# Another table for the order of all operations of a sliding-window attention and cosine-MLP kernel

## The chip, the cores and the metric

One core of one Trainium2 chip. The engines are TensorE (PE, whose weight loads are shown apart as PEld), VectorE (DVE), ScalarE (ACT), GpSimd (POOL) and SyncE (SP); the last two issue the DMAs. The metric is device time in microseconds of one execution; a lower time is better.

## The reference, cut to what matters

Sliding-window attention with ALiBi slopes over 8 batches, 8 heads, 576 positions and 64 channels, followed by a two-layer network with g = h * cos(h) over all 4608 tokens.

```python
scores = scale * np.matmul(q, k.transpose(0, 1, 3, 2))
bias = slopes[:, None, None] * (-np.abs(rel).astype(np.float32))[None, :, :]
mask = (rel >= 0) & (rel < window)
scores = np.where(mask, scores + bias[None], -1000000000.0)
attn = np.exp(scores - np.max(scores, axis=-1, keepdims=True))
attn = attn / (np.sum(attn, axis=-1, keepdims=True) + 1e-09)
attn_out = np.matmul(attn, v)
x = np.ascontiguousarray(attn_out.transpose(0, 2, 1, 3)).reshape(B * S, H * D)
h = x @ w_in
g = h * np.cos(h)
out = (g @ w_out).astype(np.float32)
```

Here window is 128, w_in is 512 x 2048 and w_out 2048 x 512.

## The kernel before, in words

The program isn't written engine by engine. The function bass_alibi_sliding__then__act_gcu_kernel (L253) records 2842 operations with `op` (L115), each with its engine, what it reads and writes, and a function that issues its instructions. Then `follow` (L160) reads a table, the string TABLE, which gives one order for all operations; `emit` (L174) deals them out to the engines in that order and puts in the semaphore waits that the reads and writes require. So the table alone sets the order on each engine and on the two queues that issue DMAs. Each entry of the table is two bytes, a step from the entry before; its low 15 bits are an operation's number, and its high bit chooses DVE for the operations that can run on ACT or DVE.

The work is tiled in attention units and in chunks of tokens.

- A batch b has nine units: head pairs 0 to 3 with query half G=0, the same with G=1, and a tail of the last 64 queries. For a unit, `scores` (L518) multiplies keys with queries on PE (L539, the tail L529), `exps` (L581) takes the exponential on ACT (L598, L590), `mask` (L603) multiplies with the table EM of decay factors on DVE (L623, L611), `pv` (L627) multiplies with v on PE (L653 and L656, tail L640 and L642), `norm` (L673) divides on DVE (L694, L696), and the result goes transposed to xT, by PE and a copy (`x_pe`, L721, matmul L742, copy L751 to L753) or by a DMA transpose of SP (`x_dma`, L757).
- Queries and keys of batches 0 and 1 are loaded by POOL's DMAs (`load_qk`, L351; `load_first_q`, L359, over SP) and transposed on PE in pieces (`qk_transposes`, L469, matmuls L483, copies L500 on ACT and L501 on DVE). For batches 2 to 7 POOL loads them as they are (`load_nat`, L381, five DMAs at L385), and SP transposes each by two DMAs (`dma_transposes`, L392, L396 and L399). The tiles of q and of k have two buffers each, used by even and odd batches.
- `load_v` (L372, DMA at L375) loads v by blocks of 128 positions, again into two buffers. `load_w_in` (L406, L407) loads w_in in four blocks of 512 columns, `load_w_out` (L412, L413) w_out in four. All are issued by POOL.
- A chunk c is 512 tokens, nine in all. Chunk 0 multiplies with w_in in halves (`moe1_half`, L964, PE at L975), the others in full (`moe1`, L782) or with seven products in place of eight (`moe1_fast`, L859, L876). ACT takes the cosine, DVE multiplies. The products with w_out are `moe2` (L1161) for chunk 0 and `moe2_fast` (L1056, L1067) after, and stores go out over SP (L1095, L1168).
- `masks` (L458) makes EM: eight exponentials on ACT (L460, one for each head) and four copies on DVE (L465, each for two heads, which waits for both).

An engine's queue is strictly in order: an instruction that waits holds all that stand behind it. This also holds for the DMAs that SP and POOL issue. A buffer that is filled again waits for those who read what was in it.

The lines of `follow` that read an entry:

```python
at = (at + lo + 256 * hi) % 65536
o = self.all[at % 32768]
if isinstance(o.fn, dict):
    e = "dve" if at >= 32768 else "act"
    o.fn, o.eng = o.fn[e], (e,)
self.order.append(o)
```

Of the kernel before, what the change touches and what calls it, by code (L numbers as in the profile page):

```python
# [27 lines left out]


TABLE = (  # L30
    'c-nPV2Y6If7JmPfH!Wo*A%PHdEHqifjs=k}tV#(GFqBXPBn4$bu`FK_%_4*%1ObV(K#D*JSt&-E!h-'
    '0xDvPKfD@{Z`QYO7kX6D^JciMYzU|;fHUhcd1+;jf_Kj&N_3_w#jJy552L+3%Pc;zlP#H-yktj(-'
    'pEjqM{ck}PJwCrB3q-'
    '{9M;&d$5qHR9WADS}~;_2H1xbO#`q+wdtgon`B>6%HyG|f?3%VnDsdnr<5N0St5ZZ)?8zmXNGD<Zg2=y6N`U+Gy?'
    '$F$*GyJWJoN!r+3anTS_iMU&FrmJy)q1{k##U*rYHRJHq^Dy35b!Y@oPU}o$A?_9;n<O%5Xs0l2&{m^^1BgNm_9P'
    '~pqObs4C1TN&{Qy{6(86~%nA#%H5NW^O=4`d2vLnc~h(_}2&mQcz_^`@$G{b79x#rnLjt-93Hcj0-'
    'yv%|m2e+*e0cZK}!+72b)WUaJT8@pXD+fk0N6bOV1gB(Si4?NA5T2-'
    '!JB(zEKr!Mj%{>;HUNYjab!Z7$qCql;L3G!CjefR+FFk(bw73vr<2ntCbb8MB)_5dQYyf6J%<J=0tY;ul(MgN&rc'
    'O0s&EiG$uIcm#Y~Vab;v#yqnaVrE7GY>V-A}Btqa`;P_Nv&jvF#{*7WM`>VMkre&#)Wy?uO_aV#gax-'
    'm{4=v5trFP6j>R?Tw2c0rY#J*M(j<PaOY>o)>#w^hUa2)xJ2kX>J~-'  # L40
    '#3SczLYEI#)13`0UMgZCvSU&r@KXVhQx8AYHOt^~S#t385v1pL)39f1&X4(!RY_VSn%~;N7Le~0Vt5k)3C!7qncH'
    'Sb_KKyP6<WQBL=(H{om`}^2hwehkBNkN1f6-'
    '=6Jf`#n1*9F&|{#~8ip5b`?XFO3>mnmKg4fqM&X#D2BXTu`vb#MxEL-'
    '2=FZh<=U!>)?uhVjo~ev?pC0h90j^d!W2#$W>Vg}3Lez;yMB~`dF58D5!*GHZ4bkokcrZJo8XMBIs3+J`c0!*&!='
    'cNak2M(+9t6%k<c;_TI5&xT-;_~SjMe)zLQ?kr-'
    '9G)}so_oZgT~!nS)>B%(>F{i(nL<%Kma6dPT_kIY8xqVGm@6sSZY)QY;}3kyZHF!JjrNbPWohF6A1kpQae^Jz>4Y'
    'nMq|4ag_#Z%abX$X0Qx{bdg5-'
    'w!C^Sy0wzSSv6YO*7!5g5KOZPW>L)jeqDWi^PVfHiNt_&bV&I7<#pb?el1f*R3lvbBscPqQM6(|M=#E!7MQtWiEo'
    '^$q8jetWg{{laSk`ID;w6<lHL!It@CI3ZRWxET-dy=6bdfZi^BN)-'
    'kx6rkxYh^Af7Y$CX%W0qP@nf!;+_cuy#JAV$$(>L5)aS8M@n1a32RRL3Yb{W0a`!VJ8|o4{JEnxs(L});p(&v8a9'  # L50
    'u_yO{KZHL$YuW?tu(Sy-'
    '!vCGTmAdZpg4wXLtycpkG<<E5@OtDZg=!_1h1+Njmjw*z0aL)7QnhFOPv(elHPlI>oe%EXgvk}suL+RHI+l!oPEe'
    'ttc)y)KY7q-'
    'GO9HpEp~!82*s>_!_J5TR{@5f%EL7h^Wh(4l4fbO%j~jd783&`#My06C4>3;+Is6L%3tT|^hYe#$tr1&iB&6{dwW'
    'wmj!;Baz_4=p8Jja_9ps>tY{=<;GUvOwSAXGq+K`;>!KNrH|ImXY(ASTzHFN^apdvpSj*r6^VK)$8H@P=`NPcPO&'
    'XkYSBhFw`irt0gqb!LQPqlVQC7VwU?z)4yP6n<)+6xUk=rH29r)HJ=#nkkufV0J5o_@v9wsQWd0@&P$WT0e*0vOC'
    'WIl=#9la*x}LDtWaQG=0xl2(#f%Kz3QWi+K|tR$xwKh#_K~ywPUk>V_~X988-'
    'dL$7M*|kTUzrMQ~>ttJm@GYT>9QFLiQ#JGHIu^Q5UX9joXGsV+1N~s5tf4rg&Z0t843@yK)VUZ;eO{vvf>bj#_<{'
    'E{YJE13lG{)N}UY3D6Y>lsCkRX4ja{$9_e$IQETy;j`zD56VwIGwJ{vRRhIkkY72;<?OL;WxyDsbjLJ`d?#gik4L'
    '%OwvOj>3X-Yk5pe`ia}jeHouYwjx-lYe?zUO*6w~{=z!E<7?VOdoJcyIBk3;YN22T&Udsl*?z2EoT*eN`VQ(2lOw'  # L60
    '$ie!%Cd#CND}y^H-5G~apWoVM#%(x$>q1=4UeA7@v$>FHVpXpRNz-`z1w9-2S&rNI|0<^yIkuIxJ1&2qr-'
    'yn-P&*BAkwbEg<YgZWM`B<Ux7!?;yxT0hEB9Poq9_H<xB+6$<+&1*V*jXQ=!i##UhbBC-HxJ9b4f>O5FQM$GVlYY'
    '0;EzOMeT$+Oi@ir?~G>em;QF`Fb7Uw0-'
    ')DSUv5QX5E;wvHsQX@ok50m+CO*%wR0XM0gH$JNq(o?|pd}rcrfU%@Ny^NS$EwY}9WNlRrb}CwAb0!CyUIkX8zeE'
    't`lBMNi5`Z9289jS-byN0#8`Z0-K46!6u51NJvfI*I<pVOKD}#Bep<(EjKAJ>#OvyA?}aT-'
    'Eb<QtZWG>gAiq@nZu|-Z>5YIIxXgTPJ-Qv8(%8OF{x~utj?J<T~4~q=Mu!G!`B%o{U^X7EYfMjy|cFw5l`KlR}P!'
    'Ka8_mW<8uzKs|eA|5Ic*_e7cdlcU3q+K^v!GU5I4-4igxj^A<ASLge=;<iQSZL!w7=WR?W#-'
    'vXhCLeN@7x(>g+{qRDABl6lLS<Fw>!h`LQKaFe(HMu)ipAva=P&;AW;|7_8}?>Xa&1&CWqRI3oTyJm0VHkMj~b-'
    'KU~R;VLVn(IO$x|2XD-#Cwa~YvoxGM@0FUnOnlZXB(9|3jhMQu{ARUV7(DVnyPJ@o)_f&pP-'
    '0v1&I@q5tK0fHEZqW2B6vpePz;Nsr3p!)OwvLraMQ%IB0%b!Fk8kvD!^ICX(d5SU`>)JBl;A)3x!^A~*gA1H!Njk'  # L70
    '9bb31AJ#9jLnSFn5nJP8V+>6WI*{{9$K=-'
    'Ii4(}ekB>9rlTbz8;dAV@$vsGY#Mm*p3)v9cI)0mEeyn;9Sk1Ej+_{IEB=6m(OWM%qp|L4FkV=POcUwRSz4?%tjO'
    '!EE7%nJVFo1y$1xLEKDW3+%V*`a_(LEi!<eA{Ja22J?)4@RI|7PRIIN8a6UkTIrQNx^0MmIX}Gdse33v8*ibI3(}'
    'Q6!`hQq7VFL0TWDyL%1z)LEb|Fqa2QJsRyz<9M$)jGC(Gyq6mu#GUiIyWiMn}lrw_vC^2CnX65Kq(JOA5auqsW#('
    'az6gPr;3Fs3vS*iFTO!lleCE-fW~K`s@;f-'
    'DuL7*vWwMFvwo)YDYK%Ys!&lL=}a$qa_Dqe_$j$%4|P%7Sk&C^p7|E-05OoaEoQU{w(_HKhuIl)N)0L6E?If-ndQ'
    'f>bOkomPRMj6=zXYB;2Fs8S$=8>KAS9bxj%$jo92RQykW$_h$ynL-'
    ';1n|B~0C{NjJ5M;#~HD{_qDyS92ASr8Q=(}$hf?wlN8Dh7U35CEE3Rb4eZHcVrLB=YO&ys+EVM&F9-'
    '>_E|awkyN8>TE$>Y^ZLfm%hXRv?#4)t*Y5EYzr4%5w1xWK3uw7gWYn<tfyI;9|8HRZ>;#t145fwkp%W<gb}oO8Vt'
    ';%~TDI391Zd3iT@kVuEmcuME+!AOkCeh?Xh408{MGRAGcvK=>2_;SOCz;Xi5FXBMh@##BcNK~)Hu608vNLvl*BDH'  # L80
# [1244 lines left out]
```

## Time and profile before

| | |
|---|---|
| median of 3 runs | 300.12 us (299.69 to 300.17) |
| the profiled execution | 299.71 us |
| its span in the profile | 298.0 us |
| granted TensorE clock | 1.0 |

In a row of a group or of the timeline stand the start or the line, the time, engine, line of the kernel, operation, tiles (out<-in) and count. A row of the chain of waits gives start, length and what ran there. A row of the waits gives who waited, for whom, the total, how often and the longest. PE durations overlap: a matmul of 512 columns is shown with some 380 ns, though the next starts 216 ns after it, so rates are read from the start-to-start spacing.

### The profile page before, as it was taken

The numbers are of one execution on the slowest core, as the hardware profiler recorded it, in microseconds if no ns is written. First come the engines' busy times: TensorE is split into PE (matmuls) and PEld (weight loads), VectorE is DVE, ScalarE is ACT, GpSimd is POOL, SyncE is SP. The second block draws the span as 40 slices with busy tenths as digits, with TensorE's granted clock in tenths as the row PEclk, the third lists the DMA queues.
The fourth block names the chain that finished last, engine by engine and source line by source line (L and its number), as shares of the span: only waits on it lengthen the run. The fifth ranks groups of instructions, "written<-read, shape, count | busy, mean of one in ns | idle before, by whom it ended". The sixth has DMA issues, their size and how long they took to land.

```text
span 298.0 us, 7278 instructions
## 1 busy us (share of the span) xinstructions
PE 287.9 (97%) x2974; PEld 205.2 (69%) x2974; DVE 262.1 (88%) x522; ACT 222.1 (75%) x318; POOL 95.2 (32%) x122
## 2 busy tenths in 40 slices
PE   2899999999999999999999999999999999999996
PEld 2678845446874586458854788547768888888884
DVE  3879877599977999899999999999999999999972
ACT  5788878689757889688777878579778758778620
POOL 7997000599642303991195005000000000000000
PEclk9999999999999999999999999999999999999999
DMA  7999999999999994999999939973131400041033
GB/s 153 173 205 208 207 169 146 180 196 155 136 175 147 130 187 90 142 173 173 169 170 133 163 85 130 159 164 74 21 79 21 150 2 0 2 141 37 10 134 106
DMA packets 147729, 37.96 MB, mean 127 GB/s; under 512 B 133360, under 2 KB 146416, under 8 KB 147696
## 3 DMA queue, kind: packets, MB, share of 16 engines
q0 software_dynamic: 99344, 18.10, 79.7%
q1 hardware_dynamic: 48352, 19.41, 34.5%
q8 instruction: 23, 0.38, 0.5%
q14 instruction: 10, 0.08, 0.1%
HBM read 36.70 MB, written 9.44 MB: 155 GB/s over the span
## 4 chain that ended last, share of the span: by engine, by line
PE 94%; DVE 2%; POOL 1%; issue 1%; ACT 1%; POOLq 0%; DVEq 0%
PE ps L1067 33%; PE ps L782 24%; PE ps L876 11%; PE ps L539 5%; PE ps L975 5%; PE ps L1161 4%; PE ps L653 3%; PE ps L656 2%; PE ps L742 2%; PE ps L483 2%; PE ps L529 1%; DVE kt L501 1%; PE ps L640 1%; PE ps L642 1%; PE ps L1138 1%
## 5 line engine op out<-in xcount | busy, mean ns | idle before, releaser
L1067 PE MATMUL ps<-w_outb,gT 128*128 128x256 f16 x512 | 82.3, 273 | 0.0
L782 PE MATMUL ps<-xT,w_inb 128*128 128x512 f16 x336 | 82.2, 379 | 0.0
L787 ACT ACTIVATE cos<-ps,halfpi 128x512 f32<-128x512 f32 x84 | 54.9, 687 | 18.9 <-PE ps L782 13.9
L598 ACT ACTIVATE p<-ps 128x768 bf16<-128x768 f32 (+1 forms) x64 | 55.6, 915 | 11.5 <-PE ps L539 9.5
L791 DVE TENSOR_TENSOR gT<-ps,cos 128x512 f16<-128x512 f32 x84 | 54.5, 686 | 5.5 <-ACT cos L787 5.1
L1067 PEld LDWEIGHTS ps<-w_outb,gT 128*128 128x128 f16 x512 | 48.2, 98 | 12.5 <-issue 1.3
L782 PEld LDWEIGHTS ps<-xT,w_inb 128*128 128x128 f16 x336 | 31.7, 98 | 31.1 <-DVE gT L791 1.5
L375 POOL DMA_DIRECT2D vp<-in_v_dram x40 | 34.3, 892 | 53.1 <-PE ps L656 35.3
L1067 PE MATMUL ps<-wsum,gsum 128*128 128x256 f16 x256 | 38.5, 273 | 0.0
L623 DVE TENSOR_TENSOR p<-p,emask 128x768 bf16<-128x768 bf16 (+1 forms) x64 | 38.0, 615 | 0.3
L385 POOL DMA_DIRECT2D qnat<-in_q_dram x30 | 25.5, 918 | 23.9 <-DMA qt<-qnat 23.9
L1052 ACT ACTIVATE ob<-ps 128x512 f32<-128x512 f32 x33 | 19.6, 598 | 13.7 <-PE ps L1067 11.2
L385 POOL DMA_DIRECT2D knat<-in_k_dram x30 | 25.7, 948 | 9.3 <-DMA kt<-knat 7.0
L1067 PEld LDWEIGHTS ps<-wsum,gsum 128*128 128x128 f16 x256 | 23.2, 98 | 4.0 <-issue 0.5
L876 PE MATMUL ps<-xT,w_inb 128*128 128x256 f16 x132 | 24.8, 273 | 0.0
L696 DVE TENSOR_TENSOR xnats<-ps,rec 128x256 f16<-128x256 f32 x56 | 21.9, 420 | 0.5
L539 PE MATMUL ps<-qt,kt 64*128 64x128 bf16 (+1 forms) x320 | 20.1, 253 | 1.3 <-DVE kt L501 1.3
L653 PEld LDWEIGHTS ps<-vp,p 128*128 128x128 bf16 x256 | 16.0, 99 | 4.3 <-issue 1.0
L653 PE MATMUL ps<-vp,p 128*128 128x65 bf16 x256 | 18.9, 196 | 0.1
L1067 PE MATMUL ps<-wsum,gT 128*128 128x256 f16 x112 | 18.1, 273 | 0.0
L539 PEld LDWEIGHTS ps<-qt,kt 64*128 64x128 bf16 x320 | 11.9, 98 | 8.6 <-issue 3.6
L1161 PE MATMUL ps<-w_outb,gT 128*128 128x512 f16 x64 | 17.6, 380 | 0.0
(111 smaller groups left out, 478.0 us busy)
## 6 DMA issues: line engine op xcount, KB each, us to landing
out_dram<-ob SPq DMA_DIRECT2D x35, 256.0 KB, 2.7
vp<-in_v_dram POOLq DMA_DIRECT2D x32, 128.0 KB, 6.9
qnat<-in_q_dram POOLq DMA_DIRECT2D x24, 128.0 KB, 7.1
knat<-in_k_dram POOLq DMA_DIRECT2D x24, 128.0 KB, 10.8
w_inb<-in_moe_w_in_dram POOLq DMA_DIRECT2D x4, 512.0 KB, 10.5
w_outb<-in_moe_w_out_dram POOLq DMA_DIRECT2D x4, 512.0 KB, 21.8
gsum<-in_q_dram POOLq DMA_DIRECT2D x1, 576.0 KB, 15.5
gsum<-in_k_dram POOLq DMA_DIRECT2D x1, 576.0 KB, 17.6
```

The source lines that it names most:

```text
L375: op("pool", [lambda e, t=t, rows=rows: e.dma_start(vp[b % 2][0:rows, t, :, 0:64], v[b, :, 128 * t:128 * t + rows, :].rearrange("h p d -> ...
L385: fns.append(lambda e, t=t, rows=rows: e.dma_start(nat[which][b % 2][0:rows, t, :, :], src[b, :, 128 * t:128 * t + rows, :].rearrange("h p ...
L539: ins = e.matmul(ps[:, banks[x], c0:c1], keys_ap(b, x, pr, kc), query_ap(b, x, pr, qb, 128 * nb), start=c0 == 0 and (b, pr, G) not in seed ...
L598: op("act", lambda e: e.activation(P[i][:, :, 0:hi], src_[:, :, 0:hi], ACTF.Exp, scale=0.125), w=held + [("P", i)], occ=920 if G else 691, ...
L623: op("dve", lambda e: e.tensor_tensor(p, p, m, ALU.mult), r=[("EM", h0), ("EM", h1)] + ([] if G else [("EM2", h1)]), w=[("P", i)], occ=600 ...
L653: ins = e.matmul(o, P[i][:, x, d0:d0 + 128], V[:, kc, h, 0:65], start=True, stop=not two)
L782: op("pe", lambda e, kc=kc: e.matmul(ps[:, bank, :], w_in[:, kc, 128 * fc:128 * fc + 128], xT[:, kc, r0:r0 + CH], start=(kc == 0), stop=(k ...
L787: op("act", lambda e: e.activation(cosb[ci][:, :], ps[:, bank, :], ACTF.Sin, bias=halfpi[:, 0:1]), r=["halfpi"], w=[("B", bank), ("cos", c ...
L791: op("dve", lambda e: e.tensor_tensor(gT[gi][:, fc, :], ps[:, bank, :], cosb[ci][:, :], ALU.mult), r=[("cos", ci)], w=[("B", bank), ("g", ...
L876: op("pe", lambda e, i=i, kc=kc: e.matmul(ps[:, bank, 256 * i:256 * i + 256], left(kc, p0 + i), right(kc), start=(start and i == 0 and kc ...
L1067: op("pe", lambda e, t=t, p=p: e.matmul(ps[:, bank, 256 * t:256 * t + 256], left(p, slice(128 * t, 128 * t + 128)), right(p), start=(start ...
L1161: op("pe", lambda e, t=t, fc=fc, bank=bank: e.matmul(ps[:, bank, :], gT[gi][:, fc, 128 * t:128 * t + 128], w_out[:, fc, :], start=(fc == 0 ...
```

## The change

The string TABLE is replaced, and one line of `follow` is edited.

```diff
 TABLE = (
-    'c-nPV2Y6If7JmPfH!Wo*A%PHdEHqifjs=k}tV#(GFqBXPBn4$bu`FK_%_4*%1ObV(K#D*JSt&-E!h-'
...
+    'c-n1N30zZG_I@8(2nkt$fCW0XRYY60(^~u2|CAZESnG-l%BHN^PyrQ(DlS+SMJj?;L_t)LML{TtEN-'
...
 )
@@
             if isinstance(o.fn, dict):
-                e = "dve" if at >= 32768 else "act"
+                e = "dve" if at >= 32768 else o.eng[0]
                 o.fn, o.eng = o.fn[e], (e,)
```

Unpacked as `follow` does it (base 85, zlib, steps of two bytes), both tables name the same 2842 operations, and 2703 of the 2842 places hold another one. Every operation with a choice has "act" as its first engine. Of these, 13 change the engine: six go from ACT to DVE, seven from DVE to ACT; among the latter is the copy of the first group of batch 0's second piece of q. Counts by engine are PE 1860 in both, ACT 304 and 305, DVE 522 and 521, POOL 70, SP 86. The switches between Exp and Sin on ACT are 14 in both.

What the prediction speaks of, by engine (u0 to u7 are batch 0's units in their order, q1/k1 its first pieces, q2/k2 its second, "a" and "b" a piece's two groups):

```
ACT, from the start
before: EM2 EM6 cast EM3 EM0 EM1 EM5 q1a k1a EM4 EM7 exp u0 exp u1 q2b exp u2 exp u3 exp u4 exp u5 exp u6 x u0 x u2 x u3
after:  EM4 EM2 cast EM3 EM0 EM5 EM7 q1a EM1 k1a EM6 exp u1 exp u0 q2a q2b exp u2 exp u3 exp u4 exp u5 exp u6 x u1 x u2 x u3
DVE, from the first cast
before: cast q1b EM(2,3) k1b EM(6,7) EM(0,1) EM(4,5) mask u0 mask u1 q2a k2b k2a mask u2 mask u3 ...
after:  cast halfpi EM(2,3) vinit EM(4,5) Pt q1b ktail k1b vinit EM(0,1) EM(6,7) mask u0 mask u1 k2a k2b mask u2 mask u3 ...
PE, after the transposes of q2 and k2
before: scores u2 u3, pv u0 u1, scores u4 u5, pv u2 u3, scores u6, x u1 u0 u3 u2, scores u7, scores tail, w_in products
after:  scores u2 u3, pv u0 u1, scores u4 u5, pv u2 u3, scores u6, x u1 u0, scores u7, x u3 u2, one w_in product, scores tail, w_in products
POOL's DMAs
before: k1 [iota] q2 k2 v1 v0 v3 wi0 v2 wi1 wi2 wi3 q k v4 wo0-3 | batch 1's v1 v0 v3 v2 | nat q2 nat k2 | nat q3 | ...
after:  k1 q2 [iota] k2 v0 v1 v2 wi0 v3 wi1 wi2 wi3 q v4 k wo0-3 | batch 1's v0 v4 v1 | batch 2's v2 | batch 1's v2 v3 | batch 2's v1 | nat q2 nat k2 | batch 2's v3 | nat q4 | batch 2's v0 | nat q3 nat k3 ...
SP's DMAs
before: ... T q2, store, T k2, 2 stores, T q3, store o1, store, T k3, x tail, T k4, T q4, 2 stores, T k5, ...
after:  ... T q2, T k2, 3 stores, store o1, store, T q3, T k3, T q4, x tail, T k4, 3 stores, T k5, ...
```

In the last two lists "nat q2" is `load_nat` of q of batch 2 and "T q2" its DMA transposes; in the first part of POOL's list q and k alone are those of batch 1. Further back on POOL and SP most DMAs have other places too. On PE, groups of `scores` that stand directly behind another kind of matmul, or `qk_transposes` that do, are one more than before: 84 changes of kind in place of 82. The last 14 operations of PE are the same, as are the last 9 of SP.

More of the change, by code (lines that the diff above doesn't have):

```diff
@@ L30 @@
 TABLE = (
-    'c-nPV2Y6If7JmPfH!Wo*A%PHdEHqifjs=k}tV#(GFqBXPBn4$bu`FK_%_4*%1ObV(K#D*JSt&-E!h-'
[L32 to L80, printed above, removed]
@@ L81 @@
-    'GHNRFy;B3gs%n{7pj$fl+x7VWHhmHY6$LK<1t&5`BViq8BRfR0)!TR`@J<FZkbrVSDq@w=+*W79u-'
-    'AsdYv9Vyey(st|R(RU84Bg0wsI(4aO|@>6G)${!)5eW-e@5K<&=Z_fWO<s>k5KMFa_g&GrXJ7L|{Z-'
-    'kIjkN?mA0G*W>_y'
+    'c-n1N30zZG_I@8(2nkt$fCW0XRYY60(^~u2|CAZESnG-l%BHN^PyrQ(DlS+SMJj?;L_t)LML{TtEN-'
+    '=}or={ij=xrGtJYe#ju4ixB_!d!xd|kBFP#MP?)L6I=R4o|&ZV5uFEjxB5rfYRjH6iE@7gPHX!oFdl#jj8$=5!IH'
+    'mO=V_M!LB6aM3_8FXtCx;_(n|2~R-;?g$i%2a9p!|`<Mm(wK=72mz-CHeM6n%67t9sTW;dkVgO{5AF4zlrpd(69Y'
+    '`@^ioX;QlKQuKSL;|H=UFOvLS1%VV#-`tM1%UjfiB`Q~r<kLS;1mDUq2ezI04*+n1salZ`mk^4c5-'
@@ new lines @@
+    '&ZsB_{tx8$Bb1!Mf@@9w@)!?@^20`K|uHT*7~_XT!GFRMu8LHq(i5xqgvJjxC)FNZe$$L|KpU>T{HC>e{jleh+0R'
+    'yavfwI1|bw0#fF?Nmwt$~(l)2jt-Vr@Zs?q(y<|+UDuwciDB=v}qSO&m^_s(~%3gA4bLe3e(0OhS;J|dcIadbIGM'
+    't#-'
+    'JRcMq#r}{q_Jvjl*K2v<I2K(Y)bZqf`en~<^#$FWSnaT^K^IIcZ&+AEI~wJk!S^2YEjqoZ!BMver~O()lUw{+1hc'
+    'QTZPs6PJs(??w3kWlJc5}&w7q}G|MNg%^a%6_@BQ@;47%tY?_OTSgQG$##gpgTJoJW2r&Yp&fA|8e0{4{6ZrY{Q6'
+    'IyYb17rrB_fzj~{*hRkw^QYQGFD?ey;O<#y`fbag}^8Xb=?WMTD~E}pv({5o{{uggsexueGD$Vi))H;zw|lpNy0<'
+    '_d)s#S#BL;i7#*8DI@Y;wr5g?;?8@#Sf5=;xwS}0sCn=MT{)^;`^SgF;AS-A5+|-'
@@ new lines @@
+    'P2IX0$Ax?CFnm4mCF#=CX6p?%kzK{>5~K34(;_ij+AcGrHL3nUfA7H#R>57pr=Z2k!AKh6|Ca_#j@bY7d4oV_^@>'
+    '1lBVJzMwhi`hDOutyeGfHy*(>~rv&<WLq~L0(vO6w5FF{dmmP+aZ!-'
+    '#ArWTpuIk|^rbyXGa3Uf_ZS0?JWf9|@5~eUPOI+%l<l&p0~mDEVC*e{i#PDN(^u3sAW)!N-'
+    's#yoqFo};jCi8twes=rkUIvCQN11Nv8|tld)>Iu@UI^|+FV+_GvXKzL%#t^Lw7zBcnZzF#OT)&W$mjcV%H|D$tP&'
+    'wyR&mAe~+qA((H4d{$;63KjH3?_e?VfCGSdW`y)`HDilW+#iF+?9*4qeRuV)D1meyFep&x&qu|i%?|ig5I~FC0S@'
+    'Cl0{pZ%5JGW*rTXV!3o$C35z9^JMmVB^Rm;iN2j1u`FW%P!lokC;874<@8`-$aa(#0DyQq%6=5C+vO_}t%X!X|$-'
@@ new lines @@
+    '&)=F|Q?V@k)ROApvdBh#Uu52gN0;q$UtS-'
+    ';3&A_x?!H%eG*7HOb~AUPe~!S{QQs!|!^;hi1tJ&*orI_j>v7k2%W2-G@qu!+?k|rg-SvGezx%u#6Ta|(hBkQj=x'
+    'Gl_Hv}@T-'
+    '*sD&nz1hts0dF>$D@(EH$ECkvXs!$1OiE1e$pOOBI+I2<(UR9&FGZ^$=Qq2UrX$dFO6!)@fC3C8W5F>2{g;g*CJ2'
+    'ZvAj+)8<2PR)`yoyH7q=#0(prXqEVEIp04Lth5?8AlBDTM-'
+    '&w@_bd4fyy#jgd4(n<kxg;Ka=DhCQl!6g~E<3jZJ65B>$zA=@gUIIa&YGZ7kz~QL_}`o7pFa^azd5!lpz&>S)yv~'
+    'lg$;{U#yNq_V;*IVDV@A2n${f;<()J(R5m<m3KpvePAuP&g%7ig*ZgFj#eOX@Hz)FMjeFLFK({u7cTr$Pc=JNBwk'
+    'U!>=7F&ZA$%TvD2V^E+Mtp0z*oD!`lEbJrV`te+Z-cK3p-'
@@ new lines @@
+    'sO@86;r$coF|u6^#Ayj!Oj&|!Dxjy3s7J9f42cFIh$!gtq~Ke%y=l1QJqd*jFfJOFkbG<9M{d6zx+uSF|7{_xr<;'
+    'w3%<JhE05rDUzD(Hd9Q1Qo7^>jOE8Q*senvi`PLNz9QX<gTjki{In6Dm$5k1jv>2Zjh)CPJ2_5k-BLciaY$SZ^-'
+    'ZbaMyzz;PR~fovBFw0FtNPeY=H;hechR_KM#Zo?e7)DOu?QqLfS`8@DF(Ax9i9&hHR!%Siyq;?yjVbk*%k+*hSvy'
+    '5$W7)&*XCr#{3%d#7CL8%CeJlXg<~1LAy+I|WvTRpQcT^Pm58R??o}YGo(QBLW|u3Lk^F0)ksE9&^uj7#)R3%$8s'
+    'LKbJPQZh`R&ymck8E+G0CfAFmTi@z8>)$WEtskY0vttP&sDn`qn-RyEWgx}-S2erFV(7~7QP0*Ha``u6#Z-'
+    'OnXa%n9PQNFULrXG0s0?|@Zp4`=BYM{j*3UswAKb-'
@@ new lines @@
+    '|gKbZ|@^qv(?@FD&}P##(rOx7H840FaY{XleGASC^`HUou1-ZC;FDvTE4sAErDML6m8$o8)-'
+    'bVRg6MR)u`85tq$DO{bmE;&v7|EmW69y?>_!HSi|E8^e>;hYVJf8KLgHRY|B-'
+    '=F&Kg_eId!96k;vR|Xm(nNFM_3(wKKVB^c#{Ke>)A`ks^KN8+!Pv0Mn-j-'
+    'w#>#KR6Gh+k$bfeD(W09Ufa6HxvFRp$@M@(qUxE_&_QgT|lacoshZi2=^@Ic41Bze2p~SqAC}@NGmaI0sIq%H4k('
+    'nu(DL8i@2`(KO$~7Q*FGbJ3xaRNj)=mEYBYF4kjmg<ZTs1Kzq@t%_N8HD*A?v3GIh+hZ38If7rn)bw)2Y;iQ3(*!'
+    'sK(}Xc|}lf={gi9LvM3u@<pPSE~;!`xmQ<l(%y+a_3P0AxLml2=$bA;v_exId?2AL;Q;2Han?EYt`=6!YzVLG2>J'
@@ new lines @@
+    '}|aFdKVFBm!Z=%_m*76aOQcjYtd=3M-'
+    'BJqbhY(q8GQB}AdGe@*DO|GA(qXD|*`n5o3a>wyc4`z64(<ec<RmVNSWnIH_LtS?(=kS#5dtvHS)E5`2Bm0ci|D3'
+    '4ft=HvRsP*$AHf3FfzrBS+*Q8?z%>54#c?guC*p6y=;3<jJDdRzB(Z-'
+    '5S18(ea<rRPj|g<Hpp^t2P9f4gb|o@mt@aY42D-'
+    ';>Iq@%Mf#`AQSfK=kZvVZ(`8DTm(2cHnB$k!LA|u4T<z5nnuJ`sqcfZaWI*i#!T=t+5_YOYq*QCH;~*Rr{fr?nNH'
+    '=3?L;Xdn`bXbPVq*hyx0edl~`f>Cz@VRiP;MxNJ#jltEZF;U^%tdg)CQ0}hV+F#@Red0T_SswymK3a(yR;xVl{xN'
+    '!BQ8DIOO{|n5hiM%xB1mOx_(aOVn=P<2e1TYgZVe|ACTM=~*voB1$<nTZ>fE!aVAR@b-'
@@ new lines @@
+    'd!%x#UC{K~+NOty6X4V%{RWdX*I~98{Y`u<0d{Y!j5O4SLJy%?WKg^kB{3%5M*{*Hhth5ip~+iU%(B*Jy2Fuc9mo'
+    'z6nCb@vrkY{;{P0)v>^D=u!yw<3(WLj(+dM~x%paXqFU^aFT3WHwPy-'
+    'rLNyx+5l$PcJazUXeiXmUqgM2JK@?(0YrCNT>!^5Mdztl9+BtMjSh+!<dFxGEsnq|Ft(a>w=5sI-MV%}ot^x+p+`'
+    'wTT0_NKPx&?4KOmX#FCh2c?#GsX~qD3-kxcXR83X{juCnY1+P($rKNX7o^#0Sh{i2ZlYjZEtSVwzdsq+c-'
+    'mU?O+%)_RR1`^bklC2WH0NvbARcZYZQIR~b7X85Tf{*=~+)6g3FjW<z$e14D5pZK0#A=Gx5RMBjSOaFe#Z!~B^cY'
+    '+l)pN=+RGgG&U8Ll1`K%#gnf8)gpTRtEhKM%Y4S-GOFP(L!*J!<HBjAYeIxokSFu-'
@@ new lines @@
+    ')!o!2kcm3IvN%$Xt2Sunr<`J#NpvrO>1pdG2AZ~7V{bAE^YCFVPy*^<SZ*0F6|hGWe^KUHcu!vce!z}Qxld6>@BR'
+    'OTU3eFu?hlb4;Jrir`QXeU9y;%4{Lh}e^_#hVPj~Y^EM)qFK9~`SX^Oj>csMlHVX;^+L|&9D>2yQqSzi=!L!H$7j'
+    '+IC44V$jFiqLI#7=LDVYh6O#IQl;68}%4%?$`Ur|f0j#$i^xhs?9Cux1n&Lx#&YYn*I*ay;Rxp<S)u^3X<p);c>|'
+    '*rRrJjN+hAQLM_xu*w!!2skst=U8xHNjJrI%XS_&B`JzMHT<N_^&c$sEhmF!r6S?3%^cc>!*GipTFzLbOvCC3*yV'
+    'y@?5$&{|B*SAJ#p;y%Kk2qn#N6LHiWDmJHV{<EdJQ`h7DXZg@)WVyJ=UyDUNnoroqrdzO&0aLB@d|US!U2+N234u'
+    '*hOlENE+dt@V?pD7zBCKHg5wD2`Mz+#<udHZg3iwX0iyx+qX~VnVSm6r39#tB_JQg<&{%22S=<wo4mZv^f9lHFi+'
@@ L84 @@
+    '{Devry3&(Vd^B#A^eoyMZ{q5`>'
 )
```

## The prediction

> **What bounds the kernel now.** I read the page's busy shares first, then its chain, then pieces of the chain in order of time, then the waits, and last the timeline of the first 18 us and of SP's queue.
>
> ```profile
> span 298.0 us, 7278 instructions
> PE 287.9 (97%) x2974; PEld 205.2 (69%) x2974; DVE 262.1 (88%) x522; ACT 222.1 (75%) x318; POOL 95.2 (32%) x122
> DMA  7999999999999994999999939973131400041033
> PE 94%; DVE 2%; POOL 1%; issue 1%; ACT 1%; POOLq 0%; DVEq 0%
> 190.76 8.63 PE ps L782 x40
> 280.00 12.51 PE ps L1067 x113
> PE ps L483 <- POOL ident L421: 5.7, 1, 5.7
> PE ps L539 <- DVE kt L501: 1.3, 2, 0.9
> PEld ps L742 <- DVE xnats L696: 2.4, 9, 0.4
> PEld ps L539 <- ACT p L598: 1.8, 9, 0.2
> PEld ps L782 <- DVE gT L791: 1.5, 6, 0.3
> ```
>
> The chain is PE for 94% of the span. Busy time alone would not show that PE is at its rate, since matmuls overlap; the spacing does: 8.63 us over 40 is 0.216 us for a matmul of 512 columns, 12.51 over 113 is 0.111 for 256. Those are the rates at which PE does nothing but stream. The matmuls themselves wait for little: 5.7 us for the identity at the start, and 1.3 us for key copies in the first 14 us. The waits of weight loads (three rows, 5.7 us together) are mostly hidden under the matmul in front of them. So a new order can't take PE's work away. It can win in the first 18 us and pick up crumbs after, and it can lose wherever something lands late. The DMA line is the other thing to see: the DMA engines are at nine tenths or more until 112 us (15 slices of 7.45 us), so DMAs are the second resource that can bind.
>
> **The change part by part.** The edited line does nothing: every operation with a choice has ACT as its first engine. Everything comes from the table. No instruction is added or removed, so PE's sum of work stays; what I work out is where PE waits.
>
> *Start.* The first transposes hang on the identity, which POOL still makes behind the same three key and query loads. I take 5.7 us as unchanged.
>
> ```profile
> 10.57 0.88 ACT L500 ACTIVATE qt<-ps 128x640 bf16<-128x640 bf16 x1
> 11.06 0.82 DVE L501 COPY qt<-ps 128x640 bf16<-128x640 bf16 x1
> 11.79 1.57 DVE L501 COPY kt<-ps 128x640 bf16<-128x640 bf16 x2
> 12.07 1.51 ACT L598 ACTIVATE p<-ps 128x768 bf16<-128x768 f32 x2 [0.62 <-PE ps L539]
> 13.50 1.04 PE L539 MATMUL ps<-qt,kt 64*128 64x256 bf16 x12 [0.38 <-DVE kt L501]
> 17.96 0.28 PE L975 MATMUL ps<-xT,w_inb 128*128 128x256 f16 x1
> ```
>
> DVE's three copies run from 11.06 to 13.36 and PE's scores at 13.50 wait for the last. The new table gives one to ACT, which idled 0.62 us there: DVE saves 0.73 us (11.79 - 11.06). It gives back 0.47, because the first two exponentials are swapped while the two masks are not, so that the first mask waits for the second exponential. The scores come 0.26 us earlier. Behind them, between 15.3 and 18.0 us, PE waits in small pieces for normalisations and copies; putting the last full scores and one w_in product ahead of those transposes fills some 0.3 to 0.5 us of this. So 0.6 to 0.8 us could be won by the first w_in products. But then the weights are late:
>
> ```profile
> L407 POOL DMA_DIRECT2D w_inb<-in_moe_w_in_dram x2: 792/794/797, 9.8 to 10.5; - x2
> DMA to landing us min/median/max: 9.6/10.5/11.4
> 19.22 0.51 PE L975 MATMUL ps<-xT,w_inb 128*128 128x256 f16 x3
> 22.13 0.49 PE L975 MATMUL ps<-xT,w_inb 128*128 128x256 f16 x3
> ```
>
> Blocks 1 and 2 of w_in land at 9.8 + 9.6 = 19.4 and 10.5 + 11.4 = 21.9 us. They stand in the same place of POOL's queue after the change, behind the same bytes. PE uses them first with the third matmul of the last two rows, at 19.44 (no time to spare) and 22.35. In the new order 0.66 and 0.22 us more of PE's work stand ahead of these uses, six and two products of 0.109 us. Block 2 then allows a gain of at most 22.35 + 0.22 - 21.95 = 0.6 us. I take **0.55**; ends: 0.6 gained, or 0.3 lost if DVE's first copies, which now stand behind a mask copy that needs the sixth exponential of the masks, come late.
>
> *Batch 1's v.* A half block (64 of 128 rows) now goes between batch 1's two first blocks.
>
> ```profile
> L375 POOL DMA_DIRECT2D vp<-in_v_dram x2: 933/934/936, 17.0 to 17.9; - x2
> DMA to landing us min/median/max: 24.7/24.7/24.7
> 43.33 0.26 PE L653 MATMUL ps<-vp,p 128*128 128x65 bf16 x3
> ```
>
> Before, they landed at 41.7 and 42.6 (0.9 apart), and PE read them at 43.33. After, the second lands half a block later, at 43.1; PE, with 0.22 us more work ahead and 0.55 won, is there at 43.0. I take **0.1** lost; ends 0 and 0.6. The other loads of the first 45 us keep their places or come with half a microsecond and more to spare.
>
> *Kinds of matmul.* In the rows of the third rival, below, the product at 102.23 is followed by scores at 102.43: 0.20 us instead of 0.109. So a group of scores behind a full product costs 0.09, and the new order has one such group more: **0.1** lost.
>
> *From 45 us on.* DVE and ACT have the same operations but for 13 copies, and the work that stands on them between PE's releases and PE's needs is as tight as before; I take 0 for their stalls, with ends -1 (some of the weight-load waits above vanish) and +1 (as many new ones). SP's and POOL's order is the third rival.
>
> Sum: 299.71 (the profiled execution; its span 298.0 and 1.7 around it) - 0.55 + 0.1 + 0.1 = 299.36. That execution was 0.41 under the median of the runs, 300.12, so in the terms of the runs **299.8 us**.
>
> **The rivals.**
>
> *First, the crumbs add up.* If after 45 us the new order also saves half of the 5.7 us minus what weight loads hide, some 0.9 us, the time is 298.9. For it: DVE, at 88%, loses one operation, and POOL's prefetches run further ahead. Against it: the matmul waits that I can see lie before 18 us.
>
> *Second, new stalls on DVE and ACT.* A mask or a normalisation that stands behind an instruction that waits longer holds the scores behind it. Six copies go to DVE (0.7 us for the two wide ones), at places where DVE is full. At 0.1 to 0.2 us a place and some eight places, +1.1: 300.9.
>
> *Third, SP's queue holds the transposes of batches 3 and 4*, and the kernel gets slower.
>
> ```profile
> 69.27 4.98 SPq L396 DMA_TRANSPOSE qt<-qnat  x1
> 74.29 1.31 SPq L399 DMA_TRANSPOSE qt<-qnat  x1
> 78.91 0.40 SPq L1095 DMA_DIRECT2D out_dram<-ob  x1
> 79.35 0.47 SPq L1168 DMA_DIRECT2D out_dram<-ob  x1
> 80.23 5.86 SPq L396 DMA_TRANSPOSE kt<-knat  x1
> 86.13 1.72 SPq L399 DMA_TRANSPOSE kt<-knat  x1
> 90.69 1.18 SPq L762 DMA_TRANSPOSE xT<-xtail  x1
> 91.92 5.89 SPq L396 DMA_TRANSPOSE kt<-knat  x1
> 97.85 1.37 SPq L399 DMA_TRANSPOSE kt<-knat  x1
> DMA to landing us min/median/max: 8.5/8.5/8.5
> 99.27 6.98 SPq L396 DMA_TRANSPOSE qt<-qnat  x1
> DMA to landing us min/median/max: 12.0/12.0/12.0
> 102.23 0.27 PE L1067 MATMUL ps<-w_outb,gT 128*128 128x256 f16 x1
> 102.43 0.28 PE L539 MATMUL ps<-qt,kt 64*128 64x256 bf16 x2
> 114.28 0.27 PE L1067 MATMUL ps<-wsum,gsum 128*128 128x256 f16 x1
> 114.49 0.29 PE L529 MATMUL ps<-qt,kt 64*128 64x64 bf16 x8
> ```
>
> Batch 3's scores begin at 102.43, batch 4's at 114.49 (the tail before them with it). The queries of batch 3 were issued at 69.27; now they stand behind the store at 78.91, which waits for PE and DVE, and then all four transposes follow each other from 79.8. With the durations of these rows (6.3 and 7.6 for batch 3; 8.3, a tail of 1.2, and 7.3 for batch 4) SP has issued the last at 79.8 + 30.7 = 110.5. Its second part, issued at 109.1, lands 8.5 later, at 117.6: 3.4 us after PE wants it at 114.2. That is the upper end. The lower comes from the DMA engines' share. They were full until 111.7 and the last wanted transpose landed at 99.3 + 12.0 = 111.3. The new order owes the same transfers by then, less two stores and a v block, so if the engines stay full it lands near 109, and PE waits for nothing. POOL's loads fill the engines while SP waits for the store, so I lean to this end. Price of the rival: +2.5 (between 0 and 3.4, with a later store behind it), time 302.3. It decides from the point where batch 4's keys land after 114.2.
>
> The Trainium skill (DMA: Bandwidth & Descriptors, "Issuing engines are not separate DMA queues") says that DMAs of all issuers run on the same 16 engines and interleave; the trace agrees, with transposes of 5.0 to 7.0 us to issue while POOL's loads run. By that rule four transposes in a row are slowed by what POOL puts beside them, which is this rival. The same page ("Latency and other measured facts") gives a transpose an effective 261 GB/s; by that figure, an estimate, the 0.59 MB of a tile takes 2.3 us and the rival has no price at all. The rows stand against it, and the rows decide.
>
> **How the numbers follow.** The forecast (299.4 to 300.4 with its own terms' ends) gets 0.42, the crumbs 0.25, the new stalls 0.13, the transposes 0.20. The time is 299.8. The range runs from the first rival's 298.9, a little under it, to the third's: 298.8 to 302.3. A measurement of this kernel can tell about 0.2%, 0.6 us, from no change, so faster means under 299.5 and slower over 300.7. Faster gets 0.30, the crumbs and the low edge of the forecast; the same 0.38; slower 0.32, the two other rivals.
>
> **What would show it.** Right: in the changed profile the first w_in product starts by some 17.3 us, the first use of block 2 falls within 0.2 us of its landing, PE's v product of batch 1 starts near 43.1, scores of batch 4 start near 114.2 with no idle PE ahead of them, and the last PE chain keeps 0.111 us a matmul. Wrong: an L483 start that isn't 5.7; a PE row with an idle of a microsecond that ends with a DMA, above all at 100 to 118 us; or a block of w_in that lands at another time than 19.4 and 21.9, since the cap on the gain rests on it.

## The result, and the profile after

| | before | after |
|---|---|---|
| median, runs of one sitting | 300.14 us (299.69 to 300.31) | 301.52 us (301.33 to 301.76) |
| the profiled execution | 299.71 us | 301.33 us |
| its span | 298.0 us | 299.6 us |

The changed kernel is slower by about half a per cent: ratio 1.0047, 95% interval 1.0033 to 1.0060. The prediction was 299.8.

Rows of the changed kernel's page (its lines are four further down than before):

```profile
span 299.6 us, 7288 instructions
PE 287.3 (96%) x2974; PEld 204.4 (68%) x2974; DVE 261.0 (87%) x521; ACT 221.6 (74%) x319; POOL 95.1 (32%) x122
...
PE 83%; DVE 9%; DMA 4%; ACT 2%; issue 1%; SPq 1%; DVEq 0%; ACTq 0%
...
L700 DVE TENSOR_TENSOR xnats<-ps,rec 128x256 f16<-128x256 f32 x56 | 21.9, 418 | 2.4 <-DMA xT<-xnats 1.8
```

PE's work is the same, but it makes 83% of the chain in place of 94%; DVE and DMA have come into it. And a group has a wait that it did not have: the normalisation, L700, idled 1.8 us for a DMA from xnats to xT. The waits of PE say who stood behind it:

```profile
PE ps L487 <- ACT gsum L372: 5.9, 1, 5.9
PE ps L657 <- DVE xnats L700: 1.2, 1, 1.2
```

PE's v products, L657, waited once for that normalisation. The timeline gives the place, on PE:

```profile
185.31 0.59 PE L786 MATMUL ps<-xT,w_inb 128*128 128x512 f16 x2
187.09 0.20 PE L657 MATMUL ps<-vp,p 128*128 128x65 bf16 x1 [1.19 <-DVE xnats L700]
...
187.58 1.24 PE L786 MATMUL ps<-xT,w_inb 128*128 128x512 f16 x5
```

Two matmuls at 0.216 us from 185.31 on leave PE free at 185.74; it goes on at 187.09, 1.35 us later. On DVE, the last reciprocal is ready at 184.48, and the normalisation waits:

```profile
184.31 0.17 DVE L698 RECIPROCAL rec<-ps 128x4 f32<-128x4 f32 x1
186.27 0.76 DVE L700 TENSOR_TENSOR xnats<-ps,rec 128x256 f16<-128x256 f32 x2 [1.79 <-DMA xT<-xnats]
```

In the kernel before, the same two rows of DVE have no wait between them:

```profile
184.28 0.24 DVE L694 RECIPROCAL rec<-ps 128x4 f32<-128x4 f32 x2
184.56 0.76 DVE L696 TENSOR_TENSOR xnats<-ps,rec 128x256 f16<-128x256 f32 x2
```

What it waits for is a buffer. The normalised tiles go round in eight:

```python
NX = 8
xnats = sb("xnats", [128, NX, 256], F16)
```

`norm` of tile n writes buffer n % 8, and `x_dma` or `x_pe` must first have read what tile n - 8 left there. Here the reader is a DMA transpose on SP that carries the result of batch 5, first head pair, second half of the queries. I call it the late transpose. SP's rows after:

```profile
175.09 2.46 SPq L772 DMA_TRANSPOSE xT<-xnats  x2
177.66 0.53 SPq L1099 DMA_DIRECT2D out_dram<-ob  x1
178.24 4.34 SPq L772 DMA_TRANSPOSE xT<-xnats  x3
```

And before:

```profile
153.91 2.47 SPq L768 DMA_TRANSPOSE xT<-xnats  x2
...
173.59 6.87 SPq L768 DMA_TRANSPOSE xT<-xnats  x4
...
197.03 1.08 SPq L1095 DMA_DIRECT2D out_dram<-ob  x2
```

After, the late transpose is the second of the three from 178.24. The first transpose of the row at 175.09 and the store at 177.66 stand ahead of it now; before, they were the first of the row at 153.91 and of the row at 197.03, and the late transpose was the third of the four from 173.59. The first of the three from 178.24, behind it before, also stands ahead of it now. The line's own view gives its issue and its landing, after:

```profile
L772 SPq DMA_TRANSPOSE xT<-xnats x1: 1244/1244/1244, 179.5 to 179.5; - x1
...
DMA to landing us min/median/max: 6.8/6.8/6.8
```

and before:

```profile
L768 SPq DMA_TRANSPOSE xT<-xnats x1: 1239/1239/1239, 177.9 to 177.9; - x1
...
DMA to landing us min/median/max: 3.4/3.4/3.4
```

It landed at 186.3 in place of 181.3: 1.6 us for its place, 3.4 for a longer way. What ran beside it after, on POOL, are the v loads of batch 7, three of them from 177.82 on:

```profile
175.08 0.88 POOL L379 DMA_DIRECT2D vp<-in_v_dram  x1 [16.67 <-PE ps L660]
177.82 2.44 POOL L379 DMA_DIRECT2D vp<-in_v_dram  x3 [1.87 <-PE ps L646]
```

### The profile page after: what moved, and what is told of

It is laid out like the page before. It is cut to its first block, busy times and chain, and to the rows that moved or that the text cites. A ratio compares the mean times of both kernels' runs of the same rounds, so it can differ in the third digit from the quotient of the medians.

```text
span 299.6 us, 7288 instructions
## 1 busy us (share of the span) xinstructions
PE 287.3 (96%) x2974; PEld 204.4 (68%) x2974; DVE 261.0 (87%) x521; ACT 221.6 (74%) x319; POOL 95.1 (32%) x122
## 4 chain that ended last, share of the span: by engine, by line
PE 83%; DVE 9%; DMA 4%; ACT 2%; issue 1%; SPq 1%; DVEq 0%; ACTq 0%
PE ps L1071 28%; PE ps L786 20%; PE ps L880 11%; PE ps L979 5%; PE ps L1165 5%; PE ps L543 4%; DVE gT L795 3%; PE ps L657 2%; DMA xT<-xnats 2%; PE ps L487 2%; PE ps L660 1%; DMA ob<-in_q_dram 1%; PE ps L746 1%; DVE p L627 1%; DVE xnats L700 1%
## 5 line engine op out<-in xcount | busy, mean ns | idle before, releaser
L1071 PE MATMUL ps<-w_outb,gT 128*128 128x256 f16 x512 | 83.4, 273 | 0.0
L1071 PE MATMUL ps<-wsum,gsum 128*128 128x256 f16 x256 | 40.4, 273 | 0.0
L1056 ACT ACTIVATE ob<-ps 128x512 f32<-128x512 f32 x31 | 18.4, 597 | 12.8 <-PE ps L1071 11.1
L700 DVE TENSOR_TENSOR xnats<-ps,rec 128x256 f16<-128x256 f32 x56 | 21.9, 418 | 2.4 <-DMA xT<-xnats 1.8
L543 PE MATMUL ps<-qt,kt 64*128 64x128 bf16 (+1 forms) x320 | 19.5, 247 | 1.7 <-DVE kt L505 1.1
L657 PEld LDWEIGHTS ps<-vp,p 128*128 128x128 bf16 x256 | 15.7, 98 | 7.0 <-DVE xnats L700 2.5
L657 PE MATMUL ps<-vp,p 128*128 128x65 bf16 x256 | 18.6, 195 | 1.8 <-DVE xnats L700 1.2
L1071 PE MATMUL ps<-wsum,gT 128*128 128x256 f16 x112 | 19.2, 273 | 0.0
## 6 DMA issues: line engine op xcount, KB each, us to landing
w_inb<-in_moe_w_in_dram POOLq DMA_DIRECT2D x4, 512.0 KB, 10.6
```

What stands on the lines that cost most here:

```text
L543: ins = e.matmul(ps[:, banks[x], c0:c1], keys_ap(b, x, pr, kc), query_ap(b, x, pr, qb, 128 * nb), start=c0 == 0 and (b, pr, G) not in seed ...
L657: ins = e.matmul(o, P[i][:, x, d0:d0 + 128], V[:, kc, h, 0:65], start=True, stop=not two)
L1071: op("pe", lambda e, t=t, p=p: e.matmul(ps[:, bank, 256 * t:256 * t + 256], left(p, slice(128 * t, 128 * t + 128)), right(p), start=(start ...
```

## The experiments

Theory: the loss is this one wait for a buffer, 1.35 us, and 0.24 more at the next v products (188.90, after five matmuls of 0.216 from 187.58). SP's order and the v loads beside it make the transpose late. Smaller terms are the half block of v and the start. Each median stands beside that of the kernel before in the same sitting. `move` is a function added behind `follow`, which takes one operation of the order ahead of another (last argument 0) or behind it (1), and all others keep their order; operations go by their number in the record, and the late transpose is 1502.

```diff
+    def move(self, a, b, behind):
+        seq = [o.seq for o in self.order]
+        o = self.order.pop(seq.index(a))
+        seq.remove(a)
+        self.order.insert(seq.index(b) + behind, o)
```

### Ten buffers in place of eight

All orders stay as in the changed kernel; the normalised tiles go round in ten buffers.

```diff
-        NX = 8
+        NX = 10
```

> The changed kernel with 10 buffers for the normalised tiles (xnats) in place of 8; every engine's order stays that of the changed kernel. Theory (the loss is a wait for a buffer: near 186 us DVE's norm may not write a buffer before a transpose that SP issued late has read it, and PE's p x v behind it waits 1.35 us, then 0.24): the 1.79 us idle time ahead of that norm is gone and the time falls by 1.3 to 1.65, from 301.5 to 299.9-300.2. Rival 1 (the late transposes cost through what they write, the xT columns for the w_in products, or through the shared DMA engines): nothing changes, 301.3-301.7. Rival 2 (the wait is one of several that end together): some 0.6 comes back, 300.9.

Measured: 299.83 us beside 300.0, ratio 0.9992 (0.9984 to 1.0001). The transposes of this run, the late one second, and behind them the normalisation:

```profile
L772 SPq DMA_TRANSPOSE xT<-xnats x2: 1180/1211/1242, 178.4 to 179.7; - x2
...
DMA to landing us min/median/max: 6.6/6.6/6.7
```

```profile
184.56 0.72 DVE L700 TENSOR_TENSOR xnats<-ps,rec 128x256 f16<-128x256 f32 x2
```

The late transpose is as late as ever (179.7 + 6.6 = 186.3). But nobody waits to write over what it reads, and by the ratios 0.55%, 1.65 us, come back. So it does not cost through the columns of xT that it writes, nor by what its lateness does to other DMAs; it costs through the buffer that it reads.

### Ten buffers in the kernel before

> The kernel before with 10 buffers for xnats, orders unchanged: what the two buffers are worth where the order of SP does not hold this wait. Theory (in the kernel before the transposes are read in time): no change, ratio 0.999 to 1.001, 300.0-300.3. Rival (the buffers are short everywhere and any order gains from two more): 0.5 to 1.5 faster, 298.6-299.6.

Measured: 299.66 beside 300.0, ratio 0.9985 (0.9975 to 0.9995). That is 0.15% faster, a little outside of what the theory expected; where it comes from stays open. It leaves most of the 0.55% of the run above to the changed order.

### The late transpose earlier on SP

Eight buffers; it goes ahead of the transpose issued at 175.09 (1255).

```diff
+        self.move(1502, 1255, 0)
```

> The changed kernel with one entry of the order moved: on SP the transpose that reads the buffer in question (batch 6, first w_in quarter, issued at 179.47 us) goes ahead of the transpose issued at 175.09, so also ahead of a store (177.66) and two other transposes. Theory (the place in SP's queue makes it late): it is issued near 174.5 and lands by 178.5-179.5, DVE's norm near 184.7 waits for nothing, 299.9-300.2. Rival 1 (the norm waits for another buffer or for data): 301.3-301.7. Rival 2 (the next transpose of the row, now issued near 179.5 and landing near 186, becomes the wait of its own norm two units on, near 187.5): 300.2-300.6.

(The text above calls it batch 6's. It carries batch 5's result; it is batch 6's normalisation that waits.) Measured: 299.89 beside 300.0, ratio 0.9991 (0.9980 to 1.0002). Its issue and landing, and the normalisation:

```profile
L779 SPq DMA_TRANSPOSE xT<-xnats x1: 1183/1183/1183, 176.1 to 176.1; - x1
...
DMA to landing us min/median/max: 4.6/4.6/4.6
```

```profile
184.90 0.73 DVE L707 TENSOR_TENSOR xnats<-ps,rec 128x256 f16<-128x256 f32 x2
```

It is issued at 176.1 and lands at 180.7, both later than expected (174.5 and 178.5 to 179.5), but still in time: the normalisation does not wait, and the transpose that was put behind it (the second rival) makes no wait of its own.

### The v loads later

SP stays as in the changed kernel; the v load issued at 177.82 (1586), with the two behind it, waits until the late transpose has landed.

```diff
+        self.move(1586, 1502, 1)
+        self.move(1585, 1586, 1)
+        self.all[1586].preds[self.all[1502]] = DATA
```

> The changed kernel with three of batch 7's v loads (issued on POOL at 177.82, 178.50 and 179.37) held until the transpose in question has landed; SP's order stays. The loads are first used after 209 us. Theory A (place in the queue and shared DMA engines each make a part of it: the transpose took 6.8 us from issue to landing beside these loads, 2.8 us shortly before them): it is issued near 179.5 and lands by 182.3-183, nothing waits, 299.9-300.3. Theory B (the place in SP's queue alone, the landing time of such a transpose does not hang on the loads): lands near 186.2, no change, 301.3-301.7.

Measured: 299.94 beside 300.0, ratio 0.9997 (0.9987 to 1.0006). The late transpose and POOL's loads:

```profile
L781 SPq DMA_TRANSPOSE xT<-xnats x1: 1795/1795/1795, 179.6 to 179.6; - x1
...
DMA to landing us min/median/max: 2.9/2.9/2.9
```

```profile
183.02 2.44 POOL L388 DMA_DIRECT2D vp<-in_v_dram  x3 [6.94 <-DMA xT<-xnats]
```

Issued at the same time as in the changed kernel, it lands in 2.9 us in place of 6.8. That is theory A: SP's order and the loads both have a part, and taking either away is enough.

### The late place alone, in the kernel before

Nothing but SP's order is edited: the transpose of 153.9 (1255) goes ahead of the one issued at 176.7 (1514), the store of 197.0 (1629) behind the addition that makes it (1628), the transpose of 179.2 (1515) behind that store, and the late transpose behind this.

```diff
+        self.move(1255, 1514, 0)
+        self.move(1629, 1628, 1)
+        self.move(1515, 1629, 1)
+        self.move(1502, 1515, 1)
```

> The kernel before, its order changed on SP alone: the transpose that DVE's norm near 184.6 us waits for (issued at 177.92, landed at 181.35 before) goes to where the changed kernel has it, behind the transpose that was issued at 153.9, the store that was issued at 197.0 and one more transpose. Nothing else moves. Theory (this place in SP's queue, beside the v loads, is enough for the whole loss): it is issued near 180 and lands at 185.5-186.5, DVE's norm and PE's p x v behind it wait 1 to 1.6 us, 301.0-301.7. Rival (the loss needs the rest of the new table too, such as the earlier v loads of batch 7): it lands before 184.6, no change, 300.0-300.3.

Measured: 305.3 beside 299.98, ratio 1.0178 (1.0160 to 1.0196). The sign is the theory's, the size three to five times its own. PE's rows:

```profile
189.23 0.23 PE L663 MATMUL ps<-vp,p 128*128 128x65 bf16 x1 [3.90 <-DVE xnats L706]
...
190.11 2.68 PE L792 MATMUL ps<-xT,w_inb 128*128 128x512 f16 x7
192.62 0.19 PE L663 MATMUL ps<-vp,p 128*128 128x65 bf16 x1
```

Stretches of the run; the granted clock is the third number from the end:

```profile
180.00:188.00 8.00, 5.33 (x90) 4.39 (x88) 4.48 (x12) 6.38 (x8) 3.08 (x4) 1.00 2.12 127
188.00:190.00 2.00, 0.77 (x15) 0.77 (x16) 1.35 (x3) 0.00 (x0) 0.00 (x0) 0.68 1.45 153
190.00:192.00 2.00, 2.00 (x11) 0.84 (x9) 1.53 (x6) 0.00 (x0) 0.00 (x0) 0.50 1.51 199
```

The transpose left at 180.4 and landed at 188.4, after 8.0 us and two to three us later than expected, so PE idled 3.9. Behind that the clock stood at half. The v products took 190.11 - 189.23 = 0.88 us where the same ones took 187.58 - 187.09 = 0.49 in the changed kernel, and seven w_in products 2.51 in place of 1.51: 1.4 us more. 3.9 and 1.4 are the 5.3.

### The same, with the v loads of batch 7 held

```diff
+        self.all[1585].preds[self.all[1502]] = DATA
```

> The kernel before with the transpose late on SP (as in the run that took 305.3: issued 180.40, landed 188.40), and batch 7's v loads held until it has landed; in that run one was issued just ahead of it (178.20) and three right behind (180.61 to 182.16). Theory A (the v loads make it land late): issued near 180, it lands by 183-184, DVE's norm near 184.6 does not wait, 300.0-300.4. Theory B (the transposes of batch 7's q, issued from 181.93 on over the same SP queue, make it late): it lands after 187 and the time stays above 303.

Measured: 303.06 beside 299.74, ratio 1.0113 (1.0100 to 1.0126). The late transpose was issued at 181.0 and landed 3.0 us after, at 184.0, and no normalisation waited for it, as theory A has it. But the time was lost again elsewhere, on PE:

```profile
192.16 0.20 PE L651 MATMUL ps<-vp,ptail 128*128 128x65 bf16 x1 [2.23 <-DMA vp<-in_v_dram]
```

I had not looked at what stood behind the held load on POOL: the half block of v of batch 6 (1260). The same profile has a wait of 1.2 us for a block of w_in near 20 us; the next run's profile has it too (1.1 us), although nothing was moved there. In a second form the half block goes ahead of the held loads.

```diff
+        self.move(1260, 1585, 0)
```

> As the run before (the kernel before with the transpose late on SP and batch 7's v loads held until it has landed, 303.06), but the half block of v of batch 6, which there stood behind the held loads on POOL, landed at 192.11 and made PE wait 2.39 us, goes ahead of them. Theory (the late place on SP costs only through the v loads beside it): the transpose lands by 184-184.8, the half block by 188, PE waits at neither, 300.0-300.6. Rival (batch 7's v blocks or the transposes of its k, now later, bring a new wait after 190): over 301.

Measured: 299.80 beside 300.12, ratio 0.9994 (0.9982 to 1.0005). The late transpose was issued at 181.1 and landed after 3.4 us, at 184.5. With the same four edits on SP as in the run of 305.3, nothing is lost: the late place costs only beside those loads.

### The half block of v, and the iota

Four runs on top of the ten buffers. First, the half block of batch 1's v (64) back behind the load of q for batch 3 that follows batch 2's v loads (372):

```diff
+        self.move(64, 372, 1)
```

> The changed kernel with 10 buffers and one more entry of the order moved: on POOL the half block of v of batch 1 goes back from its place between the first two full v blocks to behind the loads of v for batch 2, near where the kernel before has it. Theory (the half block makes the second v block land 0.6-0.7 us later and PE waits for that block near 44 us): the block lands near 43.3, the wait of 0.57-0.87 there goes to at most 0.15, and 0.4-0.6 of it stays won to the end: 299.2-299.4 (10 buffers alone: 299.83). Rival (PE then waits as long a little later, for the next v blocks or for banks): 299.7-299.9.

Measured: 302.32 beside 299.98, ratio 1.0088 (1.0053 to 1.0123). PE near 44 us, and at the tail of batch 1:

```profile
43.97 0.39 PE L1172 MATMUL ps<-w_outb,gT 128*128 128x512 f16 x1
44.19 0.26 PE L664 MATMUL ps<-vp,p 128*128 128x65 bf16 x3
...
76.79 0.24 PE L651 MATMUL ps<-vp,ptail 128*128 128x65 bf16 x1 [3.19 <-DMA vp<-in_v_dram]
```

There is no wait at 44 us (0.22 us is the product's own time), but this run does not show that the half block made it. PE came only at 44.19, behind 0.8 us of waiting for w_in near 20 us, and by then the block would have landed in the changed kernel too (43.8). And the place that I chose was wrong: in the new order it is issued at 70.4, and PE needs the half block at 73.5.

Second, the iota (4), POOL's instruction that fills the table of distances, back ahead of the load of q's second piece (9), the half block as in the changed kernel:

```diff
+        self.move(4, 9, 0)
```

> The changed kernel with 10 buffers and one more entry moved: on POOL the iota for the distances goes back ahead of the load of the second piece of q. Theory (that load, issued 0.4 us earlier on POOL, delays the landing of the first piece of q over SP by 0.24, and so ACT's cast and PE's first transposes): the first transposes start near 5.70 in place of 5.89, 0.1-0.2 faster than 10 buffers alone, 299.6-299.75. Rival (the start is made good before the first w_in product, which waits for other things): 299.8-299.9.

Measured: 299.50 beside 299.98, ratio 0.9981 (0.9971 to 0.9991). The first transposes start at 5.70 again. The time falls by 0.3 against ten buffers alone, a little more than expected, though the two intervals overlap. PE's v product of batch 1:

```profile
43.49 0.25 PE L664 MATMUL ps<-vp,p 128*128 128x65 bf16 x3
```

In this profile and that of ten buffers alone the earlier start is made good by then, later than the rival has it: the scores ahead of this product begin at 42.73, and at 42.75 with ten buffers alone. What differs is PE's wait behind them: 0.11 us, for a block that landed at 43.4 (18.6 + 24.8), in place of 0.76 for one that landed at 44.1 (18.8 + 25.3). So in these profiles the gain comes through the v loads, which left 0.2 us earlier, and not through PE's start.

Third, both, the half block still at the place that is too late:

> The changed kernel with 10 buffers and both of the moves: the half block of v back, and the iota back ahead of the second piece of q. Theory (the three costs lie at different places and add): 299.0-299.3, faster than the kernel before by 0.7-1.1. Rival (the w_in blocks or v blocks take up what the start wins): as with the half block back alone, 299.3-299.5.

Measured: 302.58 beside 299.98, ratio 1.0084 (1.0053 to 1.0116), with a wait of 3.13 us for that half block. So it went directly behind the fourth full block (63), with the ten buffers and the iota:

```diff
+        self.move(64, 63, 1)
+        self.move(4, 9, 0)
```

> The changed kernel with 10 buffers, the iota back ahead of the second piece of q, and on POOL the half block of v of batch 1 directly behind the fourth full block instead of between the first two (in the run in which it went behind batch 2's loads it landed at 76.75, after its first use near 73.4, so that place was too late). Theory (the wait near 44 us goes and nothing takes its place): the second v block lands near 42.6-43.4, the half block near 46-47, no wait over 0.2 at either, 299.1-299.4. Rival 1 (the loads behind the half block, of q's natural rows for batch 3, come 0.7 us later and hold the transposes on SP): 299.5-300. Rival 2 (the wait for the v block is small already in the run with the iota back, 0.22): 299.4-299.6, no gain over it.

Measured: 299.17 beside 299.74. By the medians that is 0.57 less; the ratio, 0.9991 (0.9977 to 1.0005), does not exclude no change. At 44 us no wait is left (the block landed at 42.7), and the view of PE's waits has none behind that. Two more buffers and one or two moves thus bring the new order level with the kernel before or 0.1 to 0.2% under it; for the run with the iota alone the interval lies under 1. But the kernel before with ten buffers stands at 0.9985, so a gain of the new order itself is not shown.

## Why the prediction was wrong

**The step that failed** is "From 45 us on": "I take 0 for their stalls", with SP's and POOL's order left to the third rival, and that one looked at the transposes of batches 3 and 4 alone. I followed SP's queue for what its transposes bring to PE, not for what they release. The 1.6 us are a buffer given back late, 70 us behind the place that I examined: DVE's wait for it, 1.79 us, is alone more than the +1 that I gave as the end. The ten buffers, the earlier place on SP and the later v loads each bring them back; the late place, beside the v loads, makes them, and more, in the kernel before. The DMA row that I showed could have sent me there: I read it up to 112 us, but it has nines again from 119 to 171 and from 179 to 194 us, where the late transpose stands. That 301.5 us lies within my range is luck, since the upper end, 302.3, came from the third rival.

**The second rival** names a normalisation that waits, but as one of some eight waits of 0.1 to 0.2 us out of DVE's own order. What came is a single wait of 1.79 us out of SP's.

**The third rival** did not come. Batch 4's scores in the changed kernel:

```profile
114.58 0.41 PE L533 MATMUL ps<-qt,kt 64*128 64x64 bf16 x16
```

They start 0.09 after the 114.49 of before, with no idle PE ahead of them. The lower end of that price, nothing, was the right one. The kind of mechanism was right, something late on SP beside POOL's loads; the place was another.

**Start.** PE's rows in the changed kernel:

```profile
5.89 1.92 PE L487 MATMUL ps<-ident,gsum 128*64 128x128 bf16 x32 [5.89 <-ACT gsum L372]
...
16.88 0.27 PE L979 MATMUL ps<-xT,w_inb 128*128 128x256 f16 x1
...
21.96 1.25 PE L979 MATMUL ps<-xT,w_inb 128*128 128x256 f16 x10
```

"5.7 us as unchanged" became 5.89. POOL's rows in the changed kernel, the use of the iota's result and the identity:

```profile
3.48 0.29 POOL L435 TENSOR_SCALAR_AFFINE_SELECT dif<-dif 128x128 f32<-128x128 f32 x1 [0.15 <-POOL dif L431]
...
5.39 0.35 POOL L425 TENSOR_SCALAR_AFFINE_SELECT ident<-ident 128x128 bf16<-128x128 bf16 x1
```

and with the iota back:

```profile
5.20 0.35 POOL L432 TENSOR_SCALAR_AFFINE_SELECT ident<-ident 128x128 bf16<-128x128 bf16 x1
```

It "still makes [it] behind the same three key and query loads", but the iota stood ahead of the second of them; now nothing lies between it and its use, POOL waits for its result, and the identity is ready at 5.74 in place of 5.55. The cast that PE's row names ends as late. The order alone does not fix this start: in the last run above, with the iota back too, POOL's memset of the identity took 0.49 us in place of 0.22, and PE started at 5.91. The first w_in product came at 16.88, inside the "by some 17.3". The cap held too, at a later time:

```profile
L411 POOL DMA_DIRECT2D w_inb<-in_moe_w_in_dram x2: 800/801/802, 9.9 to 10.7; - x2
...
DMA to landing us min/median/max: 9.7/10.6/11.5
```

Block 2 landed at 10.7 + 11.5 = 22.2, not at 21.9, and the fourth product of the row at 21.96, its first user, starts at 21.96 + 3 x 0.109 = 22.29. The gain there is 22.35 + 0.22 - 22.29 = 0.28 in place of 0.55.

**Batch 1's v** had the right mechanism and the wrong size. PE, and the three loads (block, half block, block):

```profile
43.10 0.39 PE L1165 MATMUL ps<-w_outb,gT 128*128 128x512 f16 x1
43.89 0.25 PE L657 MATMUL ps<-vp,p 128*128 128x65 bf16 x3 [0.39 <-issue]
```

```profile
L379 POOL DMA_DIRECT2D vp<-in_v_dram x3: 722/912/922, 17.2 to 18.8; - x3
...
DMA to landing us min/median/max: 25.0/25.0/25.2
```

The last of them landed at 18.8 + 25.0 = 43.8, where I had 43.1. PE is free at 43.32 and starts at 43.89: 0.57 lost in place of 0.1, inside the 0.6 of the upper end. The half block took 0.72 us to issue where I counted 0.45, the first block left 0.2 later than before, and the last was 0.3 longer on its way. The row says "issue", but the start lies 0.1 behind the landing. In the last run above, without the half block there, the wait is gone; with the half block but 0.2 us earlier loads it was 0.11.

**Kinds of matmul** (0.1) is too small for any run here to single out.

The sum, in profiled times: 299.71 - 0.28 + 0.57 + 1.35 + 0.24 = 301.59, and 301.33 was measured. Batch 4's scores, only 0.09 later than before, suggest that some 0.2 of the first loss had been made good by then. The two terms that I had make 0.3, inside the bound of no change. The term that I left out decides.

## What to carry to other kernels

When an order changes, follow each queue twice: for what a transfer brings and who reads it, and for the buffer that it releases and who writes there next. In a ring of n buffers that writer is n tiles on, and the margin is its start less the landing of the reader, 184.56 - 181.3 = 3.3 us at the place that broke here. Price that landing under the loads that the new order puts beside it, and before an instruction is held back, list what is queued behind it.
